# Holding the q and k weight loads back until the first chunk of the z2 weights has landed

## The chip, the cores and the metric

One core of one Trainium2 chip. The metric is device time in microseconds (us) of one execution. Kernels are compared only within the same rounds. Ratios are the mean time of one kernel's runs over that of the other's of the same rounds, so they aren't quite the ratio of the medians quoted. A "span" is the profiled execution from first to last instruction, about 2 us shorter than its time.

## The reference

Two branches work on the same layer-normalised input and are added to it: a dilated, windowed attention (A) and a gated MLP with a spatial mixing matrix (B).

```python
x = A_x                                   # (1, 2048, 512) bf16
xn = _layernorm(x)
return x + A(xn, A_wqkv, A_wo) + B(xn, B_w_in, B_w_sp, B_b_sp, B_w_out)
# A: qkv = xn @ wqkv; 32 heads of 16; each position attends to 8 positions, 2 apart; @ wo
# B: z = gelu(xn @ w_in); z1, z2 = halves of 896; z2 = layernorm(z2)
#    g = w_sp @ z2 + b_sp;  (z1 * g) @ w_out
```

For the first microseconds only this matters: x is cut into 16 blocks of 128 rows. A block has to be loaded (128 KB), normalised and transposed before TensorE can multiply it by anything. What TensorE does first is blocks 0 to 3 times the z2 half of `w_in`.

## The kernel before

The kernel adds tasks with what they read and write; a scheduler written in Python gives every engine a fixed order, and semaphore waits follow from reads and writes. The first loads, on SP's and ACT's queues (cuts marked `# ...`):

```python
ld_x(0, "sp");      ld_x(1, "act")
ld_win2(0, "sp");   ld_win2(1, "act")      # 128 of the 512 rows of the z2 weights each, 224 KB
ld_x(2, "sp");      ld_win2(3, "act")
ld_win2(2, "sp");   ld_x(3, "act")
for which, eng in ((0, "sp"), (1, "sp")):  # q and k weights, 512 KB each, rows of 1 KB
    dma(eng, ..., writes=[(("wq", "wk")[which], c) for c in range(4)], name="ld%s" % ("qk"[which]))
for b in range(4, min(8, NB)):
    ld_x(b, "sp")
dma("sp", ..., writes=["wv_raw"], name="ldwv")
```

VectorE's order in the first wave is fixed, too (`bn` and `ag` are the statistics of a block, `nm` its normalisation, `xt` its transpose on TensorE):

```python
bn(2); ag(2)
bn(3)            # waits for x3 ...
nm(2)            # ... and so does this
ag(3); nm(3)
# ...
for b, hf, k in u:                          # TensorE: blocks 0 and 1 times the z2 weights
    if b == 1 and hf == 0:
        xt(2, k2, range(4), ("xn", 2))      # needs nm(2)
    z2_mm(b, hf, k, (2, 3))                 # needs chunks 2 and 3
# ... xt(3), then blocks 2 and 3
plan.sequence(dv)
```

POOL also writes 16 KB of zeros to a scratch tensor at the start, with a software-generated transfer ("the write of zeros" below). Lines of the kernel that the views name: L599 loads of x, L608 z2 weights, L620 q and k weights, L663 `bn`, L673 `nm`, L682 `xt`, L634 warm-up matmuls, L743 the statistics of blocks 4 and up, L784 the q and k products, L823 the reduction of the attention products, L843 the step of VectorE that frees the bank for it, L909 the z2 products.

## Time and profile before

| | |
|---|---|
| time | 234.13 us, median of 3 (233.97 to 235.29) |
| profiled execution | 235.05 us, span 233.2 us |
| TensorE, VectorE busy | 98%, 88% |
| last x load of the first wave (x3) | issued 2.21, landed 9.57 us |
| first q product on TensorE | 15.26 us |

In the chain of waits each line is a start, a duration and what it was. In the list of waits a line has who waited for whom, then total, times and longest, in us. In DMA tables the columns are packets, MB and the share of the sixteen DMA engines. The prediction shows the lines.

### The profile page before, as it was taken

To read this page: it belongs to the slowest core of one execution; us is meant where nothing else is said; L and a number is where in the kernel's file an instruction comes from. 1 tells how busy PE (TensorE), PEld (TensorE's weight loads), DVE (VectorE), ACT (ScalarE), POOL (GpSimd) and SP (SyncE) were. 2 spreads that over 40 slices of the span, in tenths; PEclk is the share of its full clock that TensorE was granted. 3 is DMA by queue.
4 is the path that set the end of the run, shared out by engine and by line. 5 is a ranking of instruction groups with operands and counts; after the bars stand their busy time and mean duration, and the time that the engine had idled before them with its cause. 6 is when DMAs were issued, how large, how long until landed. Compare 5 with 4: busy or idle time off the path is not lost.

```text
span 233.2 us, 3304 instructions
## 1 busy us (share of the span) xinstructions
PE 228.0 (98%) x1238; PEld 111.4 (48%) x1238; DVE 205.0 (88%) x235; ACT 128.7 (55%) x235; POOL 40.4 (17%) x74
## 2 busy tenths in 40 slices
PE   8799999999999999999999999999999999999995
PEld 2244445444444556555555555454444444545442
DVE  4488997998998999999999899999999999989910
ACT  2498757894899997465573242333413433355321
POOL 4265838098005301000000000000000000000000
PEclk9999999999999999999999999999999999999999
DMA  6955999956206400359808999999999656845162
GB/s 202 358 162 102 142 241 348 190 155 185 67 22 131 139 3 0 62 118 174 258 0 176 183 214 254 291 216 306 238 303 187 140 192 127 269 98 116 43 151 67
DMA packets 76800, 38.65 MB, mean 166 GB/s; under 512 B 65132, under 2 KB 75244, under 8 KB 75760
## 3 DMA queue, kind: packets, MB, share of 16 engines
q1 hardware_dynamic: 70400, 31.63, 60.1%
q10 hardware_dynamic: 5568, 4.69, 7.2%
q0 software_dynamic: 816, 2.12, 2.8%
q8 instruction: 10, 0.16, 0.3%
q14 instruction: 6, 0.05, 0.1%
HBM read 18.49 MB, written 4.21 MB: 97 GB/s over the span
## 4 chain that ended last, share of the span: by engine, by line
PE 94%; DMA 3%; ACTq 1%; DVE 0%; ACT 0%; issue 0%
PE ps L1132 36%; PE ps L1251 16%; PE ps L784 12%; PE ps L939 10%; PE ps L909 9%; PE ps L764 6%; PE ps L823 3%; DMA arena<-in_A_x_dram 3%; ACTq L608 0%; PE ps L682 0%; DVE fpool L663 0%; ACTq L599 0%; DVE arena L673 0%; ACT arena L1093 0%
## 5 line engine op out<-in xcount | busy, mean ns | idle before, releaser
L1132 PE MATMUL ps<-arena 128*128 128x448 bf16 x448 | 90.6, 352 | 0.0
L1132 PEld LDWEIGHTS ps<-arena 128*128 128x128 bf16 x448 | 43.8, 98 | 42.8 <-ACT arena L1093 0.3
L1251 PE MATMUL ps<-arena 128*128 128x512 bf16 (+2 forms) x187 | 43.9, 366 | 0.0
L1200 DVE TENSOR_TENSOR arena<-arena 128x4096 bf16<-128x4096 bf16 x16 | 36.6, 2286 | 0.2
L810 DVE TENSOR_TENSOR arena<-arena 128x4096 bf16<-128x4096 bf16 x16 | 36.3, 2282 | 0.0
L1209 DVE TENSOR_TENSOR arena<-arena 128x4096 bf16<-128x4096 bf16 (+2 forms) x24 | 33.7, 1402 | 2.0 <-DMA arena<-arena 1.1
L1093 ACT ACTIVATE arena<-ps 128x512 bf16<-128x512 f32 (+2 forms) x23 | 13.0, 563 | 34.5 <-PE ps L1132 24.0
L784 PE MATMUL ps<-arena 128*128 128x512 bf16 x128 | 28.6, 379 | 0.0
L1251 PEld LDWEIGHTS ps<-arena 128*128 128x128 bf16 x187 | 17.9, 98 | 18.5
L909 PE MATMUL ps<-arena 128*128 128x448 bf16 x128 | 25.6, 353 | 0.8 <-DMA arena<-in_B_w_in_dram 0.8
L939 PE MATMUL ps<-arena 128*128 128x448 bf16 x128 | 24.8, 353 | 0.0
L1025 DVE TENSOR_TENSOR arena<-arena 128x1024 bf16<-128x1024 bf16 x32 | 21.0, 686 | 0.8 <-DMA arena<-in_B_w_sp_dram 0.4
L917 ACT ACTIVATE arena<-ps 128x448 bf16<-128x448 f32 x32 | 17.2, 548 | 5.7 <-PE ps L909 3.9
L784 PEld LDWEIGHTS ps<-arena 128*128 128x128 bf16 x128 | 12.3, 98 | 15.6 <-issue 1.3
L939 PEld LDWEIGHTS ps<-arena 128*128 128x128 bf16 x128 | 14.4, 114 | 10.3 <-issue 0.8
L945 ACT ACTIVATE arena<-ps 128x896 bf16<-128x896 f32 x16 | 14.4, 915 | 8.7 <-PE ps L939 8.7
L792 ACT ACTIVATE arena<-ps 128x1024 bf16<-128x1024 f32 x16 | 16.3, 1018 | 4.9 <-PE ps L784 4.4
L909 PEld LDWEIGHTS ps<-arena 128*128 128x128 bf16 x128 | 12.2, 98 | 12.8 <-DMA arena<-in_B_w_in_dram 1.2
L950 ACT ACTIVATE arena<-arena 128x896 bf16<-128x896 bf16 x16 | 15.2, 948 | 0.1
L764 PE MATMUL ps<-arena 128*128 128x512 bf16 x64 | 14.7, 379 | 0.0
L1141 ACT ACTIVATE ps<-ps,fpool 128x448 f32<-128x448 f32 x16 | 9.7, 604 | 8.2 <-PE ps L1132 7.2
L1093 ACT ACTIVATE ps<-arena 128x512 f32<-128x512 bf16 (+2 forms) x17 | 9.8, 575 | 6.5 <-ACT arena L1093 4.7
(70 smaller groups left out, 195.7 us busy)
## 6 DMA issues: line engine op xcount, KB each, us to landing
arena<-vscr SPq DMA_DIRECT2D x8, 1152.0 KB, 6.3
arena<-in_A_x_dram ACTq DMA_DIRECT2D x18, 128.0 KB, 4.2
vscr<-arena POOLq DMA_DIRECT2D x16, 128.0 KB, 3.1
arena<-in_A_x_dram SPq DMA_DIRECT2D x14, 128.0 KB, 5.8
out_dram<-arena ACTq DMA_DIRECT2D x14, 128.0 KB, 2.5
arena<-in_A_wqkv_dram SPq DMA_DIRECT2D x3, 512.0 KB, 8.1
arena<-in_B_w_in_dram SPq DMA_DIRECT2D x1, 896.0 KB, 4.8
arena<-in_B_w_out_dram SPq DMA_DIRECT2D x1, 896.0 KB, 6.2
```

What stands on the lines that cost most here:

```text
L764: last = t.matmul(bank(k), AC(off["xnT"] + dc * S + 128 * b, [[1, 128]]), AC(off["wv_raw"] + 512 * dc, [[1, 512]]), start=(dc == 0), stop= ...
L784: last = t.matmul(bank(k + which), AC(off["wqk"] + 1024 * dc + col0, [[1, 128]]), AC(off["xnT"] + dc * S + 512 * j, [[1, 512]]), start=(dc ...
L810: T("dve", lambda v: v.tensor_tensor(pbv, qb, kb, ALU.mult), reads=rd, writes=[("pb", s_)], est=c_dve(4096, 2.0), name="prod%d_%d" % (j, c ...
L909: last = t.matmul(ps[:, 512 * k: 512 * k + HF], AC(off["xnT"] + dc * S + 128 * b, [[1, 128]]), AC(off["w_in2"] + FH * dc + HF * hf, [[1, H ...
L917: T("act", lambda a: a.activation(A("z2", HF, FH * b + HF * hf), ps[:, 512 * k: 512 * k + HF], ACTF.Gelu_apprx_tanh, accum_out=Fv("s1", 1, ...
L939: last = t.matmul(ps[:, 512 * (k + hf): 512 * (k + hf) + HF], AC(off["xnT"] + dc * S + t0, [[ts, 128]]), AC(off["w_in1"] + FH * dc + HF * ...
L1025: T("dve", (lambda o_, x_, y_: lambda v: v.tensor_tensor(o_, x_, y_, ALU.subtract))(o_, x_, y_), reads=rd, writes=[wr], est=c_dve(NK * 128 ...
L1093: T("act", lambda a: a.activation(out_, in_, ACTF.Copy), reads=reads, writes=writes, est=c_act(n), name=name)
L1132: last = t.matmul(half(bk), lh(k), rh(k), start=(new and k == 0), stop=(k == NK - 1), skip_group_check=True)
L1200: T("dve", (lambda tv, iv, av: lambda v: v.tensor_tensor(tv, iv, av, ALU.mult))(tv, iv, av), reads=[("attn", j)] + ([("Ve", par)] if q < 2 ...
L1209: T("dve", (lambda o_, n: lambda v: v.tensor_tensor(o_, two(0, n), two(n, n), ALU.add))(o_, n), reads=[] if n > 512 else ["Vs", ("Ve", par ...
L1251: last = t.matmul(po, lh, rh, start=False, stop=(q == len(order) - 1), skip_group_check=True)
```

## The change

The intent: the q and k weights aren't needed before 13 us, and share the DMA engines with the first wave, which TensorE waits for. So SP waits for chunk 0 of the z2 weights before it issues them.

```diff
-                512 * 512 * 2, ("wqk", which), writes=[(("wq", "wk")[which], c) for c in range(4)],
+                512 * 512 * 2, ("wqk", which), reads=[("w_in2", 0)], writes=[(("wq", "wk")[which], c) for c in range(4)],
@@
             plan.sequence(dv)
+            sq = {t.name: t for t in plan.tasks if t.name.startswith("ld")}
+            plan.sequence([sq[n] for n in ("ldq", "ldk", "ldx4", "ldx5", "ldx6", "ldx7", "ldwv")])
```

## The prediction

> **What bounds the kernel now.** I began with the page: who is busy, and what ended last.
>
> ```profile
> PE 228.0 (98%) x1238; PEld 111.4 (48%) x1238; DVE 205.0 (88%) x235; ACT 128.7 (55%) x235; POOL 40.4 (17%) x74
> PE   8799999999999999999999999999999999999995
> ...
> PE 94%; DMA 3%; ACTq 1%; DVE 0%; ACT 0%; issue 0%
> ```
>
> TensorE is busy 98% of the 233.2 us, and 94% of the chain that ended last is TensorE. The only other part worth a name is "DMA 3%". The chain in order of time, cut to its beginning, says where that is:
>
> ```profile
> 2.21 7.35 DMA arena<-in_A_x_dram
> 9.56 0.02 issue
> 9.59 0.69 DVE fpool L663
> 10.28 0.32 DVE arena L673
> ...
> 10.65 0.40 PE ps L682 x4
> 11.05 0.76 PE ps L909 x4
> ...
> 12.23 3.03 PE ps L909 x16
> 15.26 6.91 PE ps L784 x32
> ```
>
> A load of x issued at 2.21 us (block 3, from ACT's queue) lands at 9.56. VectorE's statistics of block 3 (L663) wait for it; because VectorE runs in order, the normalisation of block 2 (L673) waits behind them, then its transpose on TensorE (L682). From 12.23 us TensorE runs on without a gap. So the change can earn something only in the first 12 us. How much TensorE lost to waits there, as its list of waits (whole run) shows:
>
> ```profile
> PE ps L634 <- PEq L1384: 0.8, 1, 0.8
> PE ps L682 <- DVE arena L673: 0.8, 2, 0.6
> PE ps L909 <- DMA arena<-in_B_w_in_dram: 0.8, 1, 0.8
> ```
>
> The first wait is the start of the program. The other two are 1.6 us, and the second of them is for rows of the z2 weights. The table by stretches counts 9.44 us busy in the first 12, of which 4.4 are warm-up matmuls.
>
> The question is whether the q and k weights are what makes x3 late. The table of DMA by stretches, for 6:7 and then 7:8 us, is the view for it (packets, MB, share; q1 is SP's queue, q10 ACT's):
>
> ```profile
> q1 hardware_dynamic: 226, 0.26, 72.8%
> q10 hardware_dynamic: 104, 0.09, 27.6%
> ...
> q1 hardware_dynamic: 347, 0.35, 100.8%
> q10 hardware_dynamic: 10, 0.01, 3.5%
> ```
>
> By 7 us q10, which carries x1, two chunks of z2 weights and x3, is nearly drained; only stragglers follow. The trace's landing records (each transfer counts up in sixteen steps) show whose they are: x3's first fifteen steps come between 6.70 and 7.92 us and the sixteenth at 9.57; z2 chunk 3 has 5.34 to 6.97, then 8.72; x2, from SP's queue, 4.77 to 5.58, then 7.80. Of z2 chunk 0 the last step is at 4.62 and only 0.05 behind the one before. So one of the sixteen engines loses about 2 us between 4.6 and 7.8, and everything after it waits for that engine. In the packet records two ACT-queue packets of 1792 bytes stand out there: 1138 ns from 4.43 and 1275 ns from 5.75, where the usual is 74 ns.
>
> And the first packet of the q weights? SP's queue brings x0 and x2 (256 packets of 1024 bytes) before them. The count of its 1024-byte packets is 255 at 6.00 us and 259 at 6.25. The q weights begin to move at about 6.1 us, after both stalls have begun.
>
> **What the Trainium skill says.** "DMA: Bandwidth & Descriptors", section "Queues, rings and completion order": every engine takes the queue rows in turn, packet by packet, and consumes one row's ring in order. So q rows queued behind chunk 2 on SP's ring can't overtake x2 or chunk 2; they can only alternate with what ACT's ring still holds. The trace agrees: 1024-byte packets of q1 start in number only when its 1792-byte ones are nearly through (240 of 256 at 6.50 us). The section "Why a DMA increments its semaphore by 16 and not by 1" says that engines finish independently and only the full count means landed; the sixteenth steps above are that. The section "Latency and other measured facts" says that engines 7 and 15 are usually slower, with the software-generated ring as a best guess only. Our trace has such a transfer, the small write of zeros from POOL (issued at 1.85, its packets from 4.88 to 7.5 us), and it coincides with the stalls; no run shows yet that it causes them. And "Issuing engines are not separate DMA queues": all queues share the same engines, which is why the change might help at all.
>
> **The change part by part.** It adds one wait on SP ahead of the q load, and fixes SP's issue order (q, k, x4 to x7, v weights), which is the order SP already has in the trace. It removes and adds no transfer and no compute instruction.
> - The release. Chunk 0 was issued at 1.25 and took 3.4 us, so 4.6. SP issues q at about 4.7 instead of 2.66: 2.0 us later.
> - When q moves. x0 was issued at 0.80 and its first packets are before 2.00: 1.2 us. So q can move from 4.7 + 1.2 = 5.9 us. It moved from 6.1 before. The wait ends just as the rings become free; I expect no hole, and no clear road either. This is the core of the prediction.
> - The rest of SP's queue. Issues cost 0.43 to 0.5 us each[...]: q 4.7, k 5.2, x4 5.7, x7 7.0, v weights 7.5. Data at 355 GB/s (the rate at 7 to 12 us) takes 1.5 us each for q and k, 0.37 for an x block: from 6.0, x4 starts at 8.9, v weights at 10.4. Every issue is ahead of that by 1.9 us or more, so the landings stay where they are (q 10.8, k 12.3, x4 12.7, v weights 15.0, by issue plus time to landing), within 0.2 us. TensorE wants q at 15.1 and the v weights at 22, so a few tenths would be hidden.
> - x3 on the late engine. Its 8 packets (8.38 to 8.97) alternate with q packets of 46 ns: 8 x 46 = 0.37 us. But q is queued there by then in the changed kernel too (5.9 < 8.4), so this isn't saved. If the stall stays, x3 still lands at about 9.5 and the change earns 0 to 0.1 us.
> - Instruction order. The scheduler that fixes each engine's order models DMA as one pipe. I worked its sums by hand: the q issue moves from 2.6 to 3.8 us, while the pipe is taken till 5.1 by the 1.44 MB ahead. So modelled landings don't move, and I expect all engines' orders to be kept.
>
> **The rivals.**
> 1. The stall comes from issuing itself: q, k and x4 to x7 are issued from 2.66 to 7.2 us, and filling rings may hold back engines (for it: the stalls lie within that time, and the x issues of SP stretch to 3.49 us for four). Then x3 would land with the other fifteen engines, at 7 to 7.9 instead of 9.6. The most TensorE can gain: 32 matmuls of the first wave at 0.19 us plus two transposes at 0.25, from 6.56 on, end at 13.1 instead of 15.26: 2.1 us. Not all of it survives: VectorE has no slack to follow. x4 lands at 12.68 and its statistics start at 12.88, so VectorE moves by 0.2 at most, and from 30 to 107 us it waits only for POOL, one load and 0.3 us for ACT. The tightest hand-over I found is the reduction at 94.98:
>
> ```profile
> 92.95 1.22 DVE L843 TENSOR_TENSOR arena<-ps,fpool 128x1024 bf16<-128x1024 f32 x1
> ...
> 94.98 0.98 PE ps L823 x16
> ```
>
> VectorE frees the bank at 94.17; with 0.15 us of hand-over TensorE could be there 0.65 earlier, 0.85 with VectorE's 0.2. So this rival makes of it a gain of about 0.9 us: 233.2. I give it 30%.
> 2. The wait starves the engines: q comes 2 us later, k and the v weights with it, and TensorE waits at q·x (15.26). Against: q has 15.1 - 10.8 = 4.3 us to spare, k 3.7, counting K's later turn. It would need a hole of over 3 us. If the x4 landing alone slips, VectorE starts its statistics later and pushes everything it gates; each tenth costs at most a tenth. Time 234.1 to 234.8; 10%.
> 3. The gain was hidden anyway (my main line, 60%): 234.1 less 0 to 0.1.
>
> **Range and chances.** 0.6 x 0.05 + 0.3 x 0.9 - 0.1 x 0.3 = 0.27 us of gain, from 234.13: 233.8 us. The three runs of before span 1.3 us (233.97 to 235.29), so a range of 232.8 to 234.7. 2% is 4.7 us, more than twice the whole 2.1 us that the opening could give, so faster by over 2% gets 0.01, slower 0.015, and within 2% the rest.
>
> **What would show each step.** q issued at about 4.7 and moving from 6.0; the sixteenth step of x3 still about 2 us behind the fifteenth, with x3 the chain's first long piece at about 7.3 us; q, k, x4 landing within 0.3 us of before; q·x (L784) on TensorE starting at 15.1 to 15.3; the same instruction order. Wrong would be: x3 landing before 8 us (rival 1; then L784 starts near 13.2, and a wait of TensorE for VectorE must show near 95), or L784 waiting for a weight load (rival 2).

## The result

233.24 us, median of 6 (232.69 to 233.62), against 234.23 of 6 (233.91 to 235.29) for the kernel before in the same rounds: ratio 0.9956, 95% interval 0.9933 to 0.9978. That is within 2%, 1.0 us faster, and a gain clear of the noise of these rounds. The instruction order of all five engines is the same as before; only line numbers are higher by 2 below the edit.

The page of the changed kernel, utilisation and chain:

```profile
PE 227.7 (98%) x1238; PEld 111.8 (48%) x1238; DVE 205.0 (89%) x235; ACT 128.5 (56%) x235; POOL 40.5 (18%) x74
...
PE 87%; DVE 8%; DMA 4%; issue 0%; ACT 0%; SPq 0%; DVEq 0%
```

TensorE does the same work. The beginning of its chain of waits, cut:

```profile
0.80 2.48 DMA arena<-in_A_x_dram
...
6.67 2.38 PE ps L911 x12
...
10.25 3.03 PE ps L911 x16
13.28 6.91 PE ps L786 x32
```

The long load of x3 is gone from it. What remains is the very first load (x0, landing at 3.28), and from 6.67 us TensorE runs without a stop: 12 matmuls where it had waited after 8. The q product starts at 13.28 instead of 15.26. The DMA tables of 6:7 and of 7:8 us, to be read against those in the prediction:

```profile
q1 hardware_dynamic: 175, 0.20, 73.7%
q10 hardware_dynamic: 98, 0.09, 25.2%
...
q1 hardware_dynamic: 328, 0.33, 102.2%
```

After 7 us ACT's queue (q10) has nothing left, where 10 stragglers had followed before. By the landing records x3's sixteen steps run from 6.50 to 7.48, the last 0.11 behind the one before it (1.65 in the kernel before). TensorE's waits over the whole run, and the hand-over near 93 us that the second line is about (the line numbers are those of the changed kernel):

```profile
PE ps L634 <- PEq L1386: 0.8, 1, 0.8
PE ps L825 <- DVE arena L845: 0.3, 1, 0.3
```

```profile
92.03 1.22 DVE L845 TENSOR_TENSOR arena<-ps,fpool 128x1024 bf16<-128x1024 f32 x1
```

```profile
93.30 1.05 PE L825 MATMUL ps<-arena 128*32 128x512 bf16 x16 [0.30 <-DVE arena L845]
```

This is the reduction that the prediction's first rival named as the tightest hand-over. TensorE lost 0.3 us of its 2.0 us lead there, and the span ended 1.7 us shorter (231.5 against 233.2).

So the picture is that of rival 1: the late engine is gone. But the change did not make q's packets begin later: by the packet records 259 packets of 1024 bytes had begun on SP's queue by 6.00 us here and by 6.25 in the kernel before, and the first 256 are x0 and x2. By 7.00 us somewhat fewer q packets had begun here (116 against 157); runs 1 and 7 below, with x3 in time whether q packets move or not, speak against that as the reason. That needed explaining.

### The profile page after: what moved, and what is told of

It reads as the page before. It is cut to its first block, busy times and chain, and to the rows that moved or that the text cites. A ratio compares the mean times of both kernels' runs of the same rounds, so it can differ in the third digit from the quotient of the medians.

```text
span 231.5 us, 3304 instructions
## 1 busy us (share of the span) xinstructions
PE 227.7 (98%) x1238; PEld 111.8 (48%) x1238; DVE 205.0 (89%) x235; ACT 128.5 (56%) x235; POOL 40.5 (18%) x74
## 4 chain that ended last, share of the span: by engine, by line
PE 87%; DVE 8%; DMA 4%; issue 0%; ACT 0%; SPq 0%; DVEq 0%
PE ps L1134 37%; PE ps L1253 16%; PE ps L786 12%; PE ps L911 8%; PE ps L766 5%; PE ps L941 5%; PE ps L825 3%; DMA arena<-in_B_w_sp_dram 2%; DVE arena L1027 1%; DMA arena<-in_A_x_dram 1%; DVE arena L883 1%; DVE arena L878 1%; DVE arena L974 1%; DVE arena L881 1%; PE ps L682 1%; DVE fpool L663 1%
```

## The experiments

The theories at the start. **A**: POOL's write of zeros stalls one DMA engine; the wait on SP has nothing to do with it. **B**: SP's early issues hold one engine back. After the first four runs: **C**: stalls strike single engines by chance, and early issues make a late engine likelier; **D**: the two profiles differ by chance alone. All runs computed the right result. Each was timed in five rounds beside the kernel before. "Landing" gives x3's last step; "q start" is the first q product on TensorE.

**1. The kernel before.** No edit.

> The kernel before, unchanged, for a second profile and for the noise of the comparison. If one engine always falls behind (both theories below need that), x3's sixteenth landing step comes 1.5 to 2.2 us after the fifteenth again, x3 lands at 9 to 10 us, and the first q product on TensorE starts at 14.8 to 15.5. If the late engine of the first profile was chance, x3 lands before 8.5 and q starts before 14. Time equal to before within 0.1%.

Measured, on chip 3: 233.52 us (233.30 to 234.24), ratio to itself 0.9992 (0.9965 to 1.0019). Its chain of waits:

```profile
0.80 2.65 DMA arena<-in_A_x_dram
...
10.61 3.03 PE ps L909 x16
13.64 6.91 PE ps L784 x32
```

There is no late engine: x3 landed at 7.95, the q product started at 13.64 and the span was 231.5, as in the changed kernel. So the 2 us of lateness in the first profile were that execution's, not the kernel's. Long packets alone don't mark a late execution: nine of 0.4 us or more stood between 4 and 7 us here (the longest 1324 ns), and eight in the first profile (the longest 1275).

**2. The changed kernel.** No edit.

> The changed kernel, unchanged, for a second profile. If the wait cures the late engine, x3 lands at 7.2 to 8 us with a last step at most 0.5 us behind, q starts at 13.0 to 13.5, and the time is 1.0 us (0.4%) below before. If the first profile was luck, x3 lands anywhere from 7.3 to 9.6.

Measured: 233.43 us (233.24 to 233.57), ratio 0.9981 (0.9953 to 1.0008), an interval that holds 1, so that this alone shows no gain; x3 at 7.98, q start 13.66 (13.0 to 13.5 was expected), span 231.5. The profile is like run 1's. What differs is the spread of the times: 0.33 us here; 1.8 us in 17 runs of the kernel before (233.30 to 235.07).

**3. The write of zeros later.** The same transfer, added after the first wave and made to wait for block 3's transpose.

```diff
-        dma("pool", ... ("vwr", 0), reads=["zeros"], writes=[("vscr", -1)], name="Vzero", prio=2)
...
         setup_masks()
+        dma("pool", ... ("vwr", 0), reads=["zeros", ("xnT", 3)], writes=[("vscr", -1)], name="Vzero", prio=2)
```

> The kernel before with one edit: POOL's small write of zeros is issued after the first wave (about 16 us instead of 1.85); the q and k loads stay early. Theory A (the software-generated transfer stalls one engine, its packets coincided with the stalls): no late engine, x3 lands by 8 us, q starts near 13.2, 233.2 us. Theory B (SP's early issues of q, k and x4 to x7 hold one engine back): nothing changes, x3 lands at about 9.5, q starts near 15.1, 234.2 us.

Measured: 233.75 us (233.28 to 234.66), ratio 1.0001 (0.9971 to 1.0031). The write was issued at 15.16, and yet in the profile

```profile
2.21 6.71 DMA arena<-in_A_x_dram
...
14.61 6.91 PE ps L780 x32
```

x3 landed at 8.92 with no software-generated packet before 16.5 us, and three of six runs were over 233.8 us. A falls: late landings come without the write. (Here x3's fifteenth step was late as well, at 8.36: more than one engine.)

**4 and 10. Half of the change: q and k early, the rest behind the wait** (the same kernel twice; the edit is shown against the changed kernel).

```diff
-                512 * 512 * 2, ("wqk", which), reads=[("w_in2", 0)], writes=...
+                512 * 512 * 2, ("wqk", which), writes=...
-                ("xin", sl), writes=[("xin", sl)], name="ldx%d" % b)
+                ("xin", sl), reads=[("w_in2", 0)] if b == 4 else [], writes=[("xin", sl)], name="ldx%d" % b)
```

> q and k are issued early as before, and only x4 to x7 and the v weights wait for the first chunk of the z2 weights. If the volume of the later issues (from 3.7 us) is what holds the engine back, x3 lands by 8 us and the time is 233.2. If it is q and k themselves (1024 rows asked for between 2.66 and 3.65 us), x3 lands at about 9.5 and the time is 234.2. Theory A expects the second as well.

> q and k early and the rest behind the wait, a second time for more runs (one of six over 233.8 so far). If q and k are the part that matters, 2 or 3 of six over 233.8; if the x and v loads are, none or one. Whatever x3's landing L is in the profile, if it is at 7.9 or later the q product starts at L + 5.69 and the span is L + 223.6.

Measured: 233.39 us (233.03 to 234.57), ratio 0.9987 (0.9957 to 1.0016), then 233.83 us (233.35 to 234.55), ratio 1.0012 (0.9991 to 1.0032). In the first profile x3 lands at 8.03, a tenth of a microsecond later than in run 1. Four of the twelve runs are over 233.8, three of them in run 10, where 2 or 3 were expected if q and k are the part that matters. In the second profile the late engine is there before anything but the first wave moves: z2 chunk 0 has its fifteenth step at 4.80 and its last at 6.09, and x3 lands at 8.37.

**5 and 6. Both kernels a third time**.

> The kernel before again, in another call (and perhaps on another chip), since its second profile showed no late engine. Theory C (stalls of about 1 us hit single engines by chance while the first 1.4 MB load, and early q, k and x loads make it likelier that one engine is hit twice): a spread of over 1 us in its runs, x3's landing in this profile anywhere from 7.8 to 9.6, and the span of the profiled run 231.5 us plus what x3 is later than 8.0. Theory D (the first pair of profiles differed by chance alone): the same spread in both kernels and equal medians.

> The changed kernel again beside it. Theory C: spread of its runs below 0.6 us, none more than 0.5 above its lowest, median 0.1 to 1.0 us below before; x3 lands by 8.1. Theory D: as wide as before and no difference in the medians.

Measured: 233.85 us (233.30 to 235.08), ratio 1.0002 (0.9977 to 1.0027), and 233.16 us (232.94 to 233.75), ratio 0.9973 (0.9951 to 0.9994). The late engine came back in the profile of the kernel before,

```profile
2.20 7.33 DMA arena<-in_A_x_dram
...
12.20 3.03 PE ps L909 x16
15.22 6.91 PE ps L784 x32
```

in an execution of 235.08 us with a span of 233.1. More than one engine was late in it: x3's fourteenth and fifteenth steps came at 8.39 and 8.90, the last at 9.53. The changed kernel's x3 landed at 7.39, its span was 231.2 and its chain has

```profile
10.30 3.03 PE ps L911 x16
13.33 6.91 PE ps L786 x32
```

D falls: the changed kernel's mean is lower by 0.27%, its interval clear of 1. One part of C's expectation missed: a run was 0.81 above the lowest, against 0.5 forecast.

**7. The wait put later: for x3.** The dependence is added after scheduling, so that no other order moves.

```diff
         plan.schedule(**(sched_kw or {}))
+        by_name["ldq"].deps.add(by_name["ldx3"])      # on the kernel before
```

> The same wait put later: q and all behind it wait for x3 instead of z2 chunk 0; instruction order unchanged. q issued at about 8, lands at 11.5 to 12.5, k at 13, x4 at 13.4 to 14. If the end is set by TensorE's start alone, q's product starts at 13.2 to 13.7 and the time equals the changed kernel's. If VectorE, which waits for x4, sets the pace after the first wave, its statistics of block 4 start at 13.5 or later instead of 11.8 to 12.8 and the time is 0.7 to 1.5 us above the changed kernel's.

Measured: 233.19 us (232.82 to 233.99), ratio 0.9974 (0.9952 to 0.9995): the changed kernel's time, though q landed at 12.0, k at 13.5 and x4 at 13.9. Of VectorE's waits, and of its timeline:

```profile
DVE fpool L743 <- DMA arena<-in_A_x_dram: 2.5, 1, 2.5
```

```profile
13.92 0.69 DVE L743 BATCH_NORM_STATS2 fpool<-arena 128x6 f32<-128x512 bf16 x1 [2.54 <-DMA arena<-in_A_x_dram]
...
91.97 1.22 DVE L843 TENSOR_TENSOR arena<-ps,fpool 128x1024 bf16<-128x1024 f32 x1
```

VectorE began block 4 at 13.92, 1.0 us later than in the first profile of the kernel before and 2.1 later than in the changed one. At the tight hand-over it was nevertheless 1.0 us earlier than in the former (91.97 against 92.95), and TensorE waited for it nowhere. So VectorE does have slack between 14 and 90 us, and x4's landing isn't what the end hangs on. The run shows something else, too: no q packet began before 9.06 us, and yet x3 landed at 7.98, as in run 1 (7.95), where 106 q packets had begun by 7.00. So in an execution without a late engine q's packets cost x3 nothing that these profiles show, and the intent of the change, to keep them off the shared DMA engines, isn't what it earns by.

**8. The changed kernel with x4 ahead of q and k.**

```diff
         plan.schedule(**(sched_kw or {}))
+        by_name["ldx4"].deps.add(by_name["ldw_in2_0"])
+        sp_o = plan.order["sp"]
+        sp_o.remove(by_name["ldx4"])
+        sp_o.insert(sp_o.index(by_name["ldq"]), by_name["ldx4"])
```

> The changed kernel with x4 issued ahead of q and k (behind the same wait). x4 lands at 7.5 to 9 instead of 11.8 to 12.7, so VectorE's statistics of block 4 follow the copy of block 3's transpose with no wait, at about 11. If VectorE's start at block 4 is what holds the changed kernel, the time falls by 0.3 us or more below it; if the floor is elsewhere (x5 to x7, POOL, or TensorE), it stays within 0.1.

Measured: 233.29 us (233.02 to 233.56), ratio 0.9975 (0.9956 to 0.9994), against 233.16 for the changed kernel in this call. x4 landed at 9.27 (7.5 to 9 was expected) and VectorE began block 4 at 10.94 without a wait, then waited 0.8 for the next block. Nothing was gained: q start was 13.32 and the span 231.2, like run 6's. Together with run 7 this settles that VectorE's start on block 4, moved here between 10.94 and 13.92 us, doesn't set the time.

**9. The other half: x4 to x7 and the v weights early, q and k behind them and the wait.**

```diff
+        by_name["ldq"].deps.add(by_name["ldw_in2_0"])  # on the kernel before, after scheduling
+        # ldq and ldk taken out of SP's order and put back behind ldwv
```

> The other half of the change: x4 to x7 and the v weights are issued early (from 2.66), and q and k behind them, after z2 chunk 0 has landed. If q and k's early issue is what makes late engines likelier, no run is over 233.8 and x3 lands by 8.1; if it is any early issue on SP's queue, about 4 in 10 runs are over 233.8 as in the kernel before (15 of 34 so far). q lands by 12, k by 13.5, which TensorE needs at 13.2 and 14.1.

Measured: 233.41 us (233.07 to 234.51), ratio 0.9996 (0.9971 to 1.0022); x3 at 8.20. One of six runs over 233.8. Inconclusive: one in six fits neither forecast well. q landed at 12.46 and k at 13.97, both 0.5 us later than forecast, yet the q product started 5.69 us after x3, so the weights weren't what it waited for.

**11. x3 late on purpose.** x3 is moved from ACT's queue to SP's, behind q.

```diff
         plan.schedule(**(sched_kw or {}))
+        x3 = by_name["ldx3"]
+        plan.order["act"].remove(x3)
+        sp_o = plan.order["sp"]
+        sp_o.insert(sp_o.index(by_name["ldq"]) + 1, x3)
```

> The kernel before with x3 moved on purpose from ACT's queue to SP's, behind q: it lands when q has moved, at 9.5 to 11. If x3's landing alone sets the end, the q product starts 5.69 us after it, the span is the landing + 223.6, no run is below 234.5, and the time is 1 to 3 us above the kernel before. If VectorE or a later stage makes it up, the span is less than landing + 223.3.

Measured: 234.89 us (234.41 to 237.18), ratio 1.0071 (1.0037 to 1.0105), span 233.0.

```profile
9.46 0.69 DVE fpool L663
...
15.18 6.86 PE ps L784 x31
```

x3 landed at 9.44. The landing plus 5.69 is 15.13 (where the chain has TensorE released), and plus 223.6 is 233.04. One run was below the 234.5 forecast as the least; without the run of 237.18 us at the lower clock the ratio is still about 1.005. z2 chunk 2 had landed at 7.34, so x3 alone was late. A late x3, made by hand, costs what it costs by chance.

**12. Block 2 normalised before the statistics of block 3.** The kernel before, one swap in VectorE's order after scheduling.

```diff
+        dve_o = plan.order["dve"]
+        dve_o.remove(by_name["norm2"])
+        dve_o.insert(dve_o.index(by_name["bnst3"]), by_name["norm2"])
```

> The kernel before, no wait on SP, with one swap on VectorE: block 2 is normalised before the statistics of block 3, so that a late x3 no longer holds block 2's transpose. If x3's late landing costs time only through that order, a late engine now costs about half (what is left is z2 chunk 2, which landed at 8.97 in the late profiles): the spread of the runs is below 0.9 us, none over 234.2, the median 233.1 to 233.5, and with x3 landing at L later than 8.5 the q product starts before L + 5.3. If the whole first wave is late in those executions, nothing changes: runs to 235, and L + 5.69. In a good execution the swap may cost up to 0.3 us, as VectorE then waits for POOL between.

Measured: 233.54 us (233.30 to 234.70), ratio 1.0005 (0.9980 to 1.0030).

```profile
2.21 5.85 DMA arena<-in_A_x_dram
...
13.62 6.85 PE ps L784 x31
```

x3 landed at 8.07 and q followed 5.5 us later instead of 5.69. But a run of 234.70 was there, above the 234.2 allowed. This one run speaks against the swap as a replacement for the wait. It may be that more than VectorE's order is late in such an execution, as z2 chunk 2 was in the late profiles (last step at 8.99 and 8.97); that isn't shown. No late profile of this kernel was caught, so the share of each stays open.

**What the profiles say together.** The columns are x3's landing, q start and span; start of the q product and span follow x3 from 7.95 us on, and below that the time lies in TensorE's own work.

| Profile | x3 | q start | span |
|---|---|---|---|
| before, first | 9.57 | 15.26 | 233.2 |
| before, third (5) | 9.53 | 15.22 | 233.1 |
| x3 behind q (11) | 9.44 | 15.13 | 233.0 |
| zeros late (3) | 8.92 | 14.61 | 232.5 |
| q and k early, second (10) | 8.37 | 14.06 | 231.9 |
| rest early (9) | 8.20 | 13.89 | 231.8 |
| block 2 first (12) | 8.07 | 13.57 | 231.4 |
| q and k early, first (4) | 8.03 | 13.72 | 231.6 |
| wait for x3 (7) | 7.98 | 13.68 | 231.5 |
| after, second (2) | 7.98 | 13.66 | 231.5 |
| before, second (1) | 7.95 | 13.64 | 231.5 |
| x4 first (8) | 7.57 | 13.32 | 231.2 |
| after, first | 7.48 | 13.28 | 231.5 |
| after, third (6) | 7.39 | 13.33 | 231.2 |

Of the ten rows from x3 = 7.95 up that have the old order on VectorE, each has q start at x3 + 5.68 to 5.70 and span at q start + 217.8 to 217.9. Of all fourteen rows the one that breaks the second sum is the first profile of the changed kernel, by its 0.3 us wait at the reduction.

And the times, counted with a line at 233.8 us that I drew after seeing the runs 1 to 8, so it is a description and not a test: of the kernel before 23 of 56 runs lie above it, of the changed kernel none of 12, of the two variants that hold q and k back as well (7 and 8) one of 12. On the chip where both ran most, the kernel before has a mean of 233.82 us in 34 runs and the changed kernel 233.32 in 12; the 19 runs of the former below the line have a mean of 233.44, so most of the difference is the slow executions. In the first comparison, on a chip I can't name, all six runs of before were above the line and none of six of the changed kernel.

No version beats the changed kernel clearly; the wait for x3 and x4 first are within 0.13 us of it.

## Why the prediction was right or wrong

**The time** was inside the range (233.24 in 232.8 to 234.7). The forecast gain was 0.27 us (234.13 - 0.27 is 233.86, which the prediction writes as 233.8); the measured one was 0.99 in the first comparison, and later ones gave ratios of 0.9981 and 0.9973, which is 0.4 and 0.6 us. That the time fell into the range is in part luck: 233.8 was an average over rivals, the range was as wide as the spread of before, and the main line (60%), 234.0 to 234.1, didn't come true.

**Right, but for some landings.** TensorE from the first q product on is one block of work and the opening is all there is to gain: the span was q start + 217.9 in profile after profile. q was issued at 4.83 (forecast 4.7), was moving by 6.0 (5.9), and left no hole. q and k landed at 9.99 and 11.44, 0.8 us earlier than in the late first profile and 0.6 later than in the good one of run 1 (9.35 and 10.83), where within 0.2 or 0.3 of before was forecast; that was hidden. The instruction order was kept. That the swing could be at most 2.1 us held: 2.0.

**The step that failed** is "If the stall stays, x3 still lands at about 9.5 and the change earns 0 to 0.1 us", with its weight of 60%. It took the late engine as a property of the kernel. The second profile of the same kernel had x3 at 7.95, and the third at 9.53. I had the hint: the profiled execution was at 235.05, when a median of 234.13 stood on the same page. A reading of the packet records can't tell a fixed delay from a chance one; a second execution can. The two long packets that the prediction reads as the stall are no proof either, since run 1 has as long ones with x3 in time.

**The step before it** was true and led astray: q's packets do begin only at 6 us, after the stalls. From this I concluded that early q loads can't matter to them. The counts say that the early loads do matter, and runs 1 and 7 speak against q packets in x3's way as the path: none of 12 changed runs is over 233.8 us, 23 of 56 of before are.

**Rival 1** had the outcome: x3 at 7 to 7.9 (7.48), q product near 13.2 (13.28), a wait for VectorE near 95 (0.3 at 93.30, in one of the three profiles of the changed kernel), a gain of 0.9 (0.99). Its argument for 0.9 out of 2.1 is not upheld. It held that VectorE has no slack and starts block 4 at most 0.2 earlier. In the changed profile it started at 11.82, 1.06 earlier; in run 7 it started 1.0 later than before and cost nothing; in run 8 it started at 10.94 and gained nothing. The better reason for about 1.0 instead of 2.0 is that the kernel before loses the 2 us in a part of its executions only. This is argued from the spread of times and the late and good profiles, not shown; no unprofiled run shows its own landings.

**x4's landing** was to stay within 0.3 us. Against the first profile it came 0.9 earlier (11.80 against 12.67), since the late engine was gone; against the good profile of run 1 it came 0.6 later (11.20). The wait has that price, and run 7 shows that an even higher one is hidden. x7 and the v weights were issued at 7.84 and 8.38, 0.8 and 0.9 later than forecast, and the "1.9 us or more" of lead doesn't follow from the prediction's own figures: k issued at 5.2, plus the 1.2 us to first data, leaves 1.1 before its turn at 7.5.

**What stays open.** Why single packets stall, and by what path early issues raise the odds of a late engine. q and k early with the rest behind the wait still gives 4 slow runs of 12, so q and k early is enough to leave the trouble; whether the x and v loads alone would is undecided at 1 of 6. Put together, in these experiments, with the same line drawn afterwards and chips mixed, 2 of 30 runs with q and k held back are over it (the changed kernel, 7, 8 and 9) and 31 of 80 with q and k early (the kernel before, 3, 4, 10 and 12); that points at q and k.

## What to carry to other kernels

Before explaining a late transfer, look where the profiled execution lies among the timed ones, and take a second profile: a delay that comes in part of the executions looks exactly like a fixed one in a single trace. Loads that aren't needed yet can be held back behind the first loads at no cost as long as they still land in time: in run 7 q landed at 12.0, 1.7 us before its product began, and even a pause in the transfers cost nothing. Here holding them back bought 0.2 to 0.4%, mostly by removing the slow executions. When a chain is one engine's work without a gap, find its start time: in 13 of 14 profiles the end was that start plus a constant to 0.1 us.

## What the Trainium skill lacked or had wrong

- "DMA: Bandwidth & Descriptors", section "Latency and other measured facts", has engines 7 and 15 as usually slower and the software-generated ring as a best guess for the reason. The records here don't say which engine is late, but with the software-generated write moved to 15 us x3 still landed at 8.92, and three of six runs were over 233.8 us (run 3). The guess isn't supported for this delay.
- No page of those I read says that an engine, or a few of them, can fall 1 to 2 us behind in one execution and not in the next of the same kernel: x3's last step at 9.57, 7.95 and 9.53 in three profiles of the kernel before.
- No page of those I read gives stalls of single packets (the table in that section of "DMA: Bandwidth & Descriptors" has a row on memory latency under load, but nothing on packets): 1792-byte packets that take 74 ns as a rule took up to 1.4 us (1415 ns at 4.5 us in run 7), and packets of 0.4 us or more stood between 4 and 7 us in 13 of the 14 profiles (not in run 10's, whose late engine shows no such packet).
- The same page's "Queues, rings and completion order" (packet-wise turns, order within a ring) agreed with the records: q's rows came in number only when chunk 2's were nearly through (some 240 of the 256 packets of chunks 0 and 2 by 6.50 us in the first profile). It didn't suffice to judge a later load harmless.
